# Lightning attention feeding a GELU MLP: second score pair of group 2 four blocks later, loads asked for one pair less far ahead, later visits moved by one to four blocks

## The chip, the cores and the metric

The kernel runs on one core of a Trainium2 chip. The metric is the device time of one execution in microseconds (us). The kernel before has a median of 215.11 us over 6 runs, from 213.0 to 217.37 us.

## The reference

Two stages follow each other. The first is a causal linear attention with decay over 4 batches, 8 heads, 768 positions and 64 features; the second is a two-layer MLP over the 3072 tokens that come out of it:

```python
# attention, per block of positions; Dmask[i, j] = lam^(i-j) where i >= j, else 0
intra    = (q_b @ k_b^T * Dmask) @ v_b
inter    = (q_b * lam^(pos+1)) @ kv_state
out_b    = intra + inter
kv_state = lam^block * kv_state + (k_b * lam^(block-1-pos))^T @ v_b
# MLP: x is the attention output as (3072, 512)
h   = x @ w_in                       # (3072, 2048)
out = gelu_exact(h) @ w_out          # (3072, 512)
```

All inputs and the output are float32. The kernel computes in bf16 with float32 accumulation.

## The kernel before, in words

**Tiling.** The sequence is cut into 6 pieces of 128 positions. A piece of one batch is a chunk (128 positions, all 8 heads), numbered n = piece x 4 + batch, 24 in all. The four chunks of a piece make up group g = 0 to 5, and the MLP works on a whole group (512 tokens) at once.

**The MLP as a list of blocks.** `mlp_blocks(g)` gives the MLP of a group as a list of blocks, each a run of TensorE matmuls. A first-layer block (L263) is 4 matmuls of 128x512 for one of 16 slices of the hidden layer, with a GELU on ScalarE behind it (L265). A second-layer block (L275) is 4 matmuls of a sum of 16; after four blocks ScalarE copies one of the four output tiles (L280) and SyncE stores it (L281). Groups 2 to 4 have 16 + 16 = 32 blocks, group 1 has 33. In groups 2 to 4 the four stores of a group follow blocks 19, 23, 27 and 31; in group 1 they follow blocks 20, 24, 28 and 32.

**Attention as visits.** The attention of group g+1 is done inside the MLP of group g. `visits[(g, i)]` (L432 on) holds what is emitted just ahead of block i. For groups 1 to 4 the line L435 gives four block numbers: at `a0` the scores of the group's first two chunks (`pair_a`, L197), at `a1` those of the other two, at `b` the `quad_b` of all four (inter-chunk part L224, intra-chunk part L230, and a copy into x_t, L236), at `st` the new states (`kv`: matmul L209, then two VectorE operations, L216 and L217). TensorE runs its instructions in the order written, so a visit that isn't ready holds up all blocks behind it.

**What a score needs.** From chunk 8 on, k and q are transposed by DMA. `request(n)` (L366) puts on SyncE's queue a transpose of k (L188) and one of q_hat (L190), and on GpSimd a multiplication q_hat = q * powers of lam (L189). `requests(n)` (L422) does so for chunks n and n+1, then puts on GpSimd their two decayed k (L169, needed only at `st`), and then calls `prefetch`, which issues loads of k, q and v for chunks up to a given number (L66; a cast from float32 to bf16, also issued by GpSimd). So GpSimd's queue is a fixed order of multiplications and load issues, and SyncE's queue a fixed order of transposes and output stores. Both run ahead of TensorE as far as their data and free buffers let them. `requests` is called for chunks 10 and 11 at block 8 of group 1, and after that at blocks `a1 + 1` (for the next group's first pair) and `b + 1` (for its second pair) of groups 1 to 3.

**Buffers.** There are 12 buffers for each of q, k and v; 6 each for q_hat, kT, qT and masked scores; 8 for decayed k; 6 for output tiles. PSUM is split into 4 banks for the MLP ("m") and 4 for attention ("sc"); scores, o_ps and kv_ps take the "sc" banks in turn, each freed by VectorE reading it.

**The start.** Before the MLP of group 0, `keep_warm` (L324) puts matmuls on a constant tile between the first chunks' visits; the last call, L354, emits three of them. The first block of group 0 needs the first slice of w_in, and later ones further slices, which are still being loaded.

Of the kernel before, what the change touches and what calls it, by code (L numbers as in the profile page):

```python
# [15 lines left out]
def kernel(  # L16
# [23 lines left out]
    M = B  # L40
# [23 lines left out]
    def load(n, name):  # L64
        raw[n, name] = qkv_pool.tile([128, H, D], BF16, tag=name, name=f"{name}_t")
        nc.gpsimd.dma_start(raw[n, name], chunk_of(name, n))  # L66
# [89 lines left out]
    def bank(shape, dtype, tag, name):  # L156
        return ps.tile(shape, dtype, tag=tag, name=name, bufs=4)
# [7 lines left out]
    def decay_k(c, eng):  # L165

        if c.so < NB - 1:
            c.k_dec = work_pool.tile([128, H, D], BF16, tag="kd", name="k_dec", bufs=8)
            eng.tensor_mul(c.k_dec, c.k, lam_m[:, :, None].to_broadcast((128, H, D)))  # L169
# [22 lines left out]
    def scores(c):  # L192
        sc_ps = [bank([128, HP, C], F32, "sc", f"sc_ps{hi}") for hi in range(2)]
        for hp in range(HP):
            for hi in range(2):
                p = slice(hi * D, (hi + 1) * D)
                nc.tensor.matmul(sc_ps[hi][:, hp, :], c.kT[p, hp, :], c.qT[p, hp, :], start=True, stop=True)  # L197
        c.sc_m = work_pool.tile([128, HP, 2, C], BF16, tag="sc_m", name="sc_m")
        dmask_r = dmask.rearrange("p (hp hi) i -> p hp hi i", hi=2)
        for hi in range(2):  # L200
            nc.vector.tensor_mul(c.sc_m[:, :, hi, :], sc_ps[hi], dmask_r[:, :, hi, :])  # L201
# [117 lines left out]
    def keep_warm(n, new=True):  # L319

        if new:
            idle_ps[0] = bank([128, 512], F32, "m", "idle_ps")
        for _ in range(n):
            nc.tensor.matmul(idle_ps[0], idle[:, :128], idle, start=True, stop=True)  # L324
# [26 lines left out]
    transposes(live[3])  # L351
    keep_warm(3)
    scores(live[3])
    keep_warm(3)  # L354
    for n in range(M):
        decay_k(live[n], nc.vector)
    make_lam_blk()
# [8 lines left out]
    def request(n):  # L366
        begin(n)
        dma_transposes(live[n])
# [3 lines left out]
    def prefetch(upto):  # L372
        while next_load[0] <= min(upto, NCH - 1):
            for name in "kqv":
                load(next_load[0], name)
            next_load[0] += 1

    def kv(*ns):
        for n in ns:
            next_state(live[n])  # L380
            take_state(live[n])
# [29 lines left out]
    def pair_a(n):  # L411
        for c in (live[n], live[n + 1]):
            scores(c)

    def quad_b(n):
        quad = [live[n + i] for i in range(M)]
        for c in quad:
            inter(c)
        for c in quad:
            intra(c)  # L420

    def requests(n):  # L422
        for m in (n, n + 1):
            request(m)
        for m in (n, n + 1):
            decay_k(live[m], nc.gpsimd)
        prefetch(n + (4 if n == 2 * M + 2 else 5))

    def add(g, i, f):
        visits.setdefault((g, i), []).append(f)  # L430


    for g in range(1, NG - 1):
        n = (g + 1) * M
        a0, a1, b, st = {1: (10, 21, 26, 31), 2: (5, 15, 21, 27)}.get(g, (4, 11, 18, 25))  # L435
        if g == 1:
            add(g, a0 - 2, lambda n=n: requests(n + 2))
        add(g, a0, lambda n=n: pair_a(n))
        add(g, a1, lambda n=n: pair_a(n + 2))
        if g + 2 < NG:  # L440
            add(g, a1 + 1, lambda n=n: requests(n + M))
            add(g, b + 1, lambda n=n: requests(n + M + 2))
        add(g, b, lambda n=n: quad_b(n))
        add(g, st, lambda n=n: kv(n, n + 1, n + 2, n + 3))
# [37 lines left out]
```

## Time and profile before

| | |
|---|---|
| median of 6 runs | 215.11 us (213.0 to 217.37) |
| the profiled execution's own time | 215.03 us |
| its span in the profile | 213.3 us |
| TensorE matmul busy | 203.5 us, 95% of the span |
| GpSimd busy | 102.5 us, all of it before 126.1 us |
| ScalarE, VectorE busy | 87.2 us, 76.1 us |
| granted TensorE clock | full in every slice |

The profile is one execution, 1.7 us shorter than that execution's own time because the span begins with the first instruction and ends with the last. Its page gives busy time by engine, a strip of 40 slices, a chain followed back from the last instruction, and groups of instructions by line. The trace behind it answers for single lines, engines and stretches. Matmuls are pipelined: one of 128x512 shows a duration of 379 ns, but in an unbroken run they follow each other every 0.216 us (16 in 3.45 us on the chain), so a block of four takes 0.86 us. A transpose or a load shows the time of its issue on the queue; the time until its data has landed is told apart.

### The profile page before, as it was taken

The numbers are of one execution on the slowest core, as the hardware profiler recorded it, in microseconds if no ns is written. First come the engines' busy times: TensorE is split into PE (matmuls) and PEld (weight loads), VectorE is DVE, ScalarE is ACT, GpSimd is POOL, SyncE is SP. The second block draws the span as 40 slices with busy tenths as digits, with TensorE's granted clock in tenths as the row PEclk, the third lists the DMA queues.
The fourth block names the chain that finished last, engine by engine and source line by source line (L and its number), as shares of the span: only waits on it lengthen the run. The fifth ranks groups of instructions, "written<-read, shape, count | busy, mean of one in ns | idle before, by whom it ended". The sixth has DMA issues, their size and how long they took to land.

```text
span 213.3 us, 3540 instructions
## 1 busy us (share of the span) xinstructions
PE 203.5 (95%) x1446; PEld 104.7 (49%) x1471; DVE 76.1 (36%) x122; ACT 87.2 (41%) x153; POOL 102.5 (48%) x118
## 2 busy tenths in 40 slices
PE   7888999999999999997999999999999999999994
PEld 2444754556644465443465444645444644444442
DVE  3777130175392334642244544138144120000000
ACT  5663662326657111565102465211456211566121
POOL 7994433892997998999999930000000000000000
PEclk9999999999999999999999999999999999999999
DMA  8999999999999799999999991131200012100112
GB/s 88 137 150 185 207 206 189 154 209 155 177 99 117 87 161 136 185 155 127 187 198 148 213 210 37 24 99 52 98 0 0 3 49 98 49 3 0 49 49 98
DMA packets 100800, 24.48 MB, mean 115 GB/s; under 512 B 92977, under 2 KB 97841, under 8 KB 100785
## 3 DMA queue, kind: packets, MB, share of 16 engines
q0 software_dynamic: 78592, 13.51, 84.8%
q1 hardware_dynamic: 22192, 10.76, 25.0%
q8 instruction: 11, 0.18, 0.4%
q14 instruction: 5, 0.03, 0.1%
HBM read 27.27 MB, written 6.29 MB: 157 GB/s over the span
## 4 chain that ended last, share of the span: by engine, by line
PE 81%; POOL 6%; DMA 6%; DVE 3%; issue 2%; ACT 0%; POOLq 0%
PE o_ps L275 37%; PE h_ps L263 33%; DMA w_in_t<-in_moe_w_in_dram 4%; DMA qT<-q_hat 3%; PE o_ps L230 3%; PE sc_ps L197 2%; PE o_ps L224 2%; PE kv_ps L209 2%; POOL k_t L66 2%; PE o_ps L289 2%; POOL q_t L66 2%; DVE state L217 1%; POOL v_t L66 1%; DVE tmp L216 1%; POOL q_hat L189 1%
## 5 line engine op out<-in xcount | busy, mean ns | idle before, releaser
L263 PE MATMUL h_ps<-x_t,w_in_t 128*128 128x512 bf16 (+2 forms) x422 | 86.0, 355 | 1.0 <-DMA w_in_t<-in_moe_w_in_dram 0.5
L275 PE MATMUL o_ps<-w_out_t,g_t 128*128 128x512 bf16 x355 | 81.0, 379 | 1.3 <-issue 0.9
L265 ACT ACTIVATE g_t<-h_ps 128x512 bf16<-128x512 f32 (+1 forms) x99 | 57.8, 584 | 36.8 <-PE h_ps L263 36.7
L263 PEld LDWEIGHTS <-w_in_t 128*128 128x128 bf16 x432 | 39.2, 98 | 42.2 <-DMA w_in_t<-in_moe_w_in_dram 1.5
L275 PEld LDWEIGHTS <-g_t 128*128 128x128 bf16 x368 | 35.1, 98 | 40.9
L201 DVE TENSOR_TENSOR sc_m<-sc_ps,dmask 128x512 bf16<-128x512 f32 x48 | 30.0, 682 | 37.3 <-PE sc_ps L197 37.3
L280 ACT COPY o_sb<-o_ps 128x512 f32<-128x512 f32 x23 | 13.5, 585 | 72.6 <-PE o_ps L275 69.7
L66 POOL DMA_DIRECT2D k_t<-in_k_dram x24 | 22.1, 921 | 5.9 <-DMA w_in_t<-in_moe_w_in_dram 3.3
L66 POOL DMA_DIRECT2D q_t<-in_q_dram x24 | 21.7, 906 | 3.5 <-DMA w_out_t<-in_moe_w_out_dram 3.4
L66 POOL DMA_DIRECT2D v_t<-in_v_dram x23 | 21.0, 916 | 3.3 <-DMA w_out_t<-in_moe_w_out_dram 1.6
L189 POOL TENSOR_TENSOR q_hat<-q_t,lam_p 128x512 bf16<-128x512 bf16 x16 | 17.3, 1108 | 8.7 <-DMA q_t<-in_q_dram 7.0
L236 DVE CAST x_t<-o_ps 128x512 bf16<-128x512 f32 x16 | 9.9, 683 | 19.1 <-PE o_ps L230 19.1
L169 POOL TENSOR_TENSOR k_dec<-k_t,lam_m 128x512 bf16<-128x512 bf16 x16 | 16.5, 1068 | 0.0
L216 DVE TENSOR_TENSOR tmp<-kv_ps,state 128x512 f32<-128x512 f32 x16 | 10.9, 684 | 14.1 <-PE kv_ps L209 14.1
L217 DVE TENSOR_TENSOR state<-tmp,lam_blk 128x512 bf16<-128x512 f32 x16 | 12.2, 762 | 0.5
L324 PE MATMUL idle_ps<-idle 128*128 128x512 bf16 x29 | 10.6, 476 | 1.2 <-DVE idle L105 1.2
L182 DVE TENSOR_TENSOR qT<-t_ps,lam_q 128x512 bf16<-128x512 bf16 x8 | 5.5, 690 | 14.8 <-PE t_ps L176 14.7
L197 PE MATMUL sc_ps<-qT,kT 64*128 64x128 bf16 x192 | 8.4, 217 | 2.4 <-DMA qT<-q_hat 1.5
L197 PEld LDWEIGHTS <-kT 64*128 64x128 bf16 x192 | 5.7, 94 | 8.1 <-issue 6.0
L230 PE MATMUL o_ps<-sc_m,v_t 128*64 128x128 bf16 x192 | 7.9, 222 | 0.2
L230 PEld LDWEIGHTS <-v_t 128*64 128x64 bf16 x192 | 5.8, 109 | 2.8 <-issue 1.6
L181 ACT COPY kT<-t_ps 128x512 bf16<-128x512 bf16 x8 | 4.7, 586 | 4.6 <-PE t_ps L176 4.6
(41 smaller groups left out, 70.5 us busy)
## 6 DMA issues: line engine op xcount, KB each, us to landing
out_dram<-o_sb SPq DMA_DIRECT2D x23, 256.0 KB, 3.1
k_t<-in_k_dram POOLq DMA_DIRECT2D x24, 128.0 KB, 5.8
q_t<-in_q_dram POOLq DMA_DIRECT2D x24, 128.0 KB, 6.5
v_t<-in_v_dram POOLq DMA_DIRECT2D x23, 128.0 KB, 7.1
w_out_t<-in_moe_w_out_dram POOLq DMA_DIRECT2D x4, 512.0 KB, 16.7
w_in_t<-in_moe_w_in_dram POOLq DMA_DIRECT2D x2, 512.0 KB, 11.6
w_in_t<-in_moe_w_in_dram POOLq DMA_DIRECT2D x2, 384.0 KB, 8.4
v_f<-in_v_dram SPq DMA_DIRECT2D x1, 256.0 KB, 3.5
```

What stands on the lines that cost most here:

```text
L66: nc.gpsimd.dma_start(raw[n, name], chunk_of(name, n))
L169: eng.tensor_mul(c.k_dec, c.k, lam_m[:, :, None].to_broadcast((128, H, D)))
L189: nc.gpsimd.tensor_mul(q_hat, c.q, lam_p[:, :, None].to_broadcast((128, H, D)))
L197: nc.tensor.matmul(sc_ps[hi][:, hp, :], c.kT[p, hp, :], c.qT[p, hp, :], start=True, stop=True)
L201: nc.vector.tensor_mul(c.sc_m[:, :, hi, :], sc_ps[hi], dmask_r[:, :, hi, :])
L216: nc.vector.tensor_add(tmp, kv_ps, states[c.b])
L217: nc.vector.tensor_mul(new, tmp, lam_blk)
L230: nc.tensor.matmul(c.o_ps[hi * D:(hi + 1) * D, hp, :], c.v[:, 2 * hp + hi, :], c.sc_m[:, hp, hi, :], start=(c.so == 0 and hp == 0), stop=T ...
L263: nc.tensor.matmul(h_ps[:, f, :], w, x_t[:, ki, lo:hi], start=(ki == 0 and f == 0), stop=(ki == NK1 - 1), skip_group_check=True)
L265: nc.scalar.activation(g_t[:, kf:kf + n_kf, lo:hi], h_ps, ACT.Gelu)
L275: nc.tensor.matmul(om[io], g_t[:, kf, io * C:(io + 1) * C], w_out_t[:, kf, :], start=(kf == 0), stop=(kf == NK2 - 1))
L280: nc.scalar.copy(o_sb, om[io])
```

## The change

Four things are altered:

- `keep_warm` at L354 emits four matmuls, not three.
- `requests(n)` prefetches up to chunk n+3, that is, only the pair that the next `requests` will ask for. Before, it was n+4 in the first call (n = 10) and n+5 afterwards.
- In group 1, `a1` and `b` are one block later (21 to 22, 26 to 27). In group 2, `a0` is one block later (5 to 6), `a1` four (15 to 19), `b` four (21 to 25), `st` three (27 to 30).
- In groups 3 and 4, `a0` is one block later (4 to 5) and `a1`, `b` and `st` are three later (11, 18, 25 to 14, 21, 28).

`requests` moves with `a1` and `b`. In the order of SyncE's queue, this puts the transposes of chunks 16 and 17 behind the first output store of group 2, those of 18 and 19 behind its second, and those of 22 and 23 behind the first store of group 3; before, each stood one store earlier. On GpSimd, multiplications and bursts of loads change places: each burst of loads issued by `requests` is now the six loads of one pair and stands directly ahead of that pair's two q_hat.

```diff
@@ -351,7 +351,7 @@
     transposes(live[3])
     keep_warm(3)
     scores(live[3])
-    keep_warm(3)
+    keep_warm(4)
     for n in range(M):
         decay_k(live[n], nc.vector)
     make_lam_blk()
@@ -424,7 +424,7 @@
             request(m)
         for m in (n, n + 1):
             decay_k(live[m], nc.gpsimd)
-        prefetch(n + (4 if n == 2 * M + 2 else 5))
+        prefetch(n + 3)
@@ -432,7 +432,7 @@
     for g in range(1, NG - 1):
         n = (g + 1) * M
-        a0, a1, b, st = {1: (10, 21, 26, 31), 2: (5, 15, 21, 27)}.get(g, (4, 11, 18, 25))
+        a0, a1, b, st = {1: (10, 22, 27, 31), 2: (6, 19, 25, 30)}.get(g, (5, 14, 21, 28))
```

## The prediction

> **What bounds the kernel now.** I read the busy row of the page first, then the list of waits, then the stretch of the chain around the one long wait, and then the engines' timelines there.
>
> ```profile
> PE 203.5 (95%) x1446; PEld 104.7 (49%) x1471; DVE 76.1 (36%) x122; ACT 87.2 (41%) x153; POOL 102.5 (48%) x118
> ```
>
> TensorE (PE) is the bound; time can only come from its gaps or from its instructions. The list of waits has these rows for it and for GpSimd (in total, times, longest, in us):
>
> ```profile
> POOL q_hat L189 <- DMA q_t<-in_q_dram: 7.0, 4, 3.3
> ...
> PE sc_ps L197 <- DMA qT<-q_hat: 1.5, 1, 1.5
> ...
> PE h_ps L263 <- DMA w_in_t<-in_moe_w_in_dram: 0.5, 1, 0.5
> ```
>
> After the start, one matmul wait counts: 1.5 us, once, by the scores for a transposed q. The others in TensorE's timeline after it are 0.16 us each. The timeline shows where (start, duration):
>
> ```profile
> 99.62 0.40 PE L197 MATMUL sc_ps<-qT,kT 64*128 64x128 bf16 x8
> 101.55 0.40 PE L197 MATMUL sc_ps<-qT,kT 64*128 64x128 bf16 x8 [1.53 <-DMA qT<-q_hat]
> 101.88 1.04 PE L263 MATMUL h_ps<-x_t,w_in_t 128*128 128x512 bf16 x4
> ```
>
> This is group 2, block 15: chunk 14's scores go at once, chunk 15's wait 1.53 us. The chain leads back through GpSimd:
>
> ```profile
> 90.96 0.95 POOL v_t L66
> 91.91 1.07 POOL q_hat L189
> 92.99 0.92 POOL q_hat L189
> ...
> 95.60 5.81 DMA qT<-q_hat
> 101.41 0.14 issue
> 101.55 0.40 PE sc_ps L197 x8
> ```
>
> GpSimd issued nine loads from 83.96 to 91.8 (for chunks 15, 16 and 17; 14 was long loaded) before it made q_hat of 14 and 15. SyncE then needed three transposes, one after the other:
>
> ```profile
> 93.00 1.19 SPq L190 DMA_TRANSPOSE qT<-q_hat  x1
> 94.28 1.22 SPq L188 DMA_TRANSPOSE kT<-k_t  x1
> 95.60 2.29 SPq L190 DMA_TRANSPOSE qT<-q_hat  x1
> ```
>
> The last landed 5.8 us after its issue, at 101.4. From 101.55 to the end TensorE has no other wait above 0.16 us, so what is saved here should reach the end whole.
>
> **Part by part. 1, the pair four blocks later.** A block takes 4 x 0.216 = 0.86 us, so chunk 15's scores would start without the wait at 101.55 - 1.53 + 4 x 0.86 = 103.5. With qT landing at 101.4 even as it is, the wait is gone with 2.1 us to spare: -1.53 us. No matmul is added; four blocks only change places with 16 score matmuls.
>
> **2, loads one pair less far ahead.** This is the part with a price, as each pair's q_hat now waits for loads issued just ahead of it, and the next burst queues behind that wait. For three bursts of the trace I asked how long a load takes to land (issues at 83-92, 95-101 and 104-111 us):
>
> ```profile
> DMA to landing us min/median/max: 4.9/5.5/6.9
> ...
> DMA to landing us min/median/max: 4.0/7.4/8.1
> ...
> DMA to landing us min/median/max: 6.0/7.4/8.3
> ```
>
> A round on GpSimd is then: six issues (5.3 us; the second chunk's q goes out at +3.5), the landing L, one q_hat (1.04), two decayed k (2.0). Up to 83.96 nothing differs: chunk 13's q_hat waited for its own load before too. Then:
> - Burst for 14, 15 from 83.96: second q at 87.5, L = 5.5 (its own row), q_hat done 94.0. Transpose q of 15 can be issued at 94.1 (before 95.60), landing at 94.1 + 5.8 = 99.9. Needed at 103.5: 3.6 us to spare.
> - Decayed k until 96.0. Burst 16, 17: second q at 99.5, L = 7.4, q_hat done 107.9; its transpose lands about 114. Needed at group 3's block 5: before it was block 4 at 123.02, so 123.02 - 1.53 + 0.86 + 0.28 = 122.6. 8 to spare.
> - Decayed k until 109.9. Burst 18, 19: second q at 113.4, L = 7.4, q_hat done 121.8, issue 121.9, landing 127.7. Needed at block 14: 129.73 - 1.53 + 3 x 0.86 + 0.28 = 131.1. 3.4 to spare, the tightest place.
> - Bursts 20, 21 and 22, 23: q_hat done 135.9 and 147.9, transposes landed 142 and 154, needed at 154.5 and 163.0.
>
> So no new wait: 0. Bounds: three landings in a row (5.5 + 7.4 + 7.4 = 20.3) may sum to 20.3 + 3.4 = 23.7 us before TensorE waits. The largest in the windows, 6.9 + 8.1 + 8.3 = 23.3, just keep inside. Below nothing isn't possible here beyond part 1, since no other wait on q exists.
>
> The Trainium skill ("DMA: Bandwidth & Descriptors", Anatomy of one DMA) prices a load from GpSimd at about 2.0 us plus bytes over 436 GB/s: for 256 KB of float32, 2.6 us. By that rule q_hat would hardly wait, a round would be 5.3 + 2.1 + 2.0 = 9.4 us, and chunk 19's transpose would land 15 us early. By the rows a round takes 12 to 14 us. I take the rows, as these loads lie beside transposes and stores. Both give 0.
>
> **3, SyncE's order.** The transposes of 16, 17 now stand behind group 2's first store (block 19 ends about 104.5, store issued about 105.3), those of 18, 19 behind its second (about 108.7), those of 22, 23 behind group 3's first (about 137). q_hat is later than the store each time except for kT of 16: 0. What queues behind a waiting transpose is stores; the third and fourth of group 2 leave about 123 in place of some time after 116, and six output buffers cover that, as the next tile comes at 137. Stores waited in this way before too: the one row of ScalarE held up by a store (o_sb on "remote", 2.9 us) delayed no matmul. I take 0; were the buffers to run out, a wait of that size is the upper bound, and nothing here can gain.
>
> **4, the other distances.** Moves change the room that VectorE has to free "sc" banks. Group 1, `b` to `st`: 5 to 4 blocks, so the states start at 82.44 in the old times, and the last x_t copy ended at 80.96: hidden, 1.5 us left. Group 2, `b` to `st`, 6 to 5: copies ended 111.06, needed 113.4. Group 2 `st` to group 3 `a0`: 9 to 7 blocks, 6.94 us from first state matmul to first score; VectorE's four additions took 114.27 to 119.48, 5.2 us. Here a rule speaks against the change: "SBUF — State Buffer", Who interferes with whom, says that a VectorE operation with two SBUF inputs (L217 is one) contends with a GpSimd one that reads SBUF, on an exclusive lock. GpSimd now has chunk 18's and 19's q_hat at about 118 and 121, beside the states at 115 to 121. The row of L217 is 691/692/1256 ns (min, median, max): at worst +0.57. By the row two meetings add 1.1 (6.3 < 6.94); by the rule, two full waits of 1.05 add 2.1 (7.3, against 7.2 for the later banks): 0.1 us at most. I take 0. Were the cover gone, each meeting would cost up to 0.57.
>
> **5, one more warm matmul.** +0.216 us at 17 us. TensorE then waits 0.47 us for w_in (it resumes at 19.03), so the wait shrinks to 0.25 and the cost is 0; uncovered it is 0.22.
>
> **Sum.** Span 213.3 - 1.53 = 211.8; the profiled execution 215.03 - 1.53 = 213.5. It lies 0.08 under the median, so I forecast a median of 213.6 us, 0.7% less. About 1% is what a measurement of this kernel can tell from no change.
>
> **Rivals.**
> - Forecast (0.58): 213.6, own range 213.0 to 214.3 (uncovered terms of parts 3 to 5, and the wait's own spread).
> - Larger gain (0.17). Runs spread from 213.0 to 217.37, and a wait on a landing is the kind that varies. If the wait is on average 2.5 us instead of 1.53, the time is 212.6. For it: 213.0 is close to this profile without its wait. Against: the profiled execution is close to the median.
> - No gain (0.16): the wait moves, or something else is late by as much. Chunk 15's landing would have to take 5.5 + 3.6 = 9.1 us, or bank waits of part 4 add up to 1 to 2 us. 215.0, between 214.3 and 216.0. For it: distances got shorter; against: every one of them keeps room in the trace.
> - Slower (0.09): landings slow GpSimd's rounds, and group 3's second pair waits. It decides from a sum of three landings of 23.7 us; the gain is used up at 25.2 (8.4 each), and over 1% is lost from 27.4 (9.1 each). At 9.5 each, the wait is 28.5 - 23.7 = 4.8, the time 215.1 - 1.5 + 4.8 = 218.4. For it: landings grew from 5.5 to 7.4 within the trace, and loads during the weights took up to 16 us. Against: no load from 83 us on needed over 8.3, and bursts are shorter now.
>
> **Range and chances.** The bulk is the forecast and half of each neighbour: 212.2 to 215.9 leaves out the slower case and the ends of two others. Faster by over 1% (under 213.0): the larger gain and a sliver of the forecast, 0.21. Slower by over 1%: 0.09. Within: 0.70.
>
> **What would show it.** Right: no score wait on qT in group 2; q_hat waiting for q_t in every round, with GpSimd's last one ending near 148 rather than 126; TensorE's first second-layer block of group 2 1.5 us plus the moved pair's 0.55 us earlier. Wrong: a wait of L197 at group 3's block 14, a wait of L197 or L209 on VectorE, or a longer gap at 19 us.

## The result and the profile after

The changed kernel has a median of 213.33 us over 17 runs (212.89 to 214.27), the kernel before 214.94 us over 36 runs (213.0 to 218.81). The ratio is 0.9937, with a 95% interval from 0.9918 to 0.9957: 1.6 us or 0.6% less. Here and below the medians are over all runs and the ratios over those in the chip's faster state alone, so a ratio is not exactly the quotient of two medians. The profiled execution took 213.22 us, with a span of 211.5 us (before 215.03 and 213.3). The runs also lie much closer together than before: 1.4 us from first to last in place of 5.8, from half as many runs.

The page's busy row, for the changed kernel:

```profile
PE 203.9 (96%) x1447; PEld 105.4 (50%) x1472; DVE 76.3 (36%) x122; ACT 87.3 (41%) x153; POOL 102.4 (48%) x118
```

The work is the same; the span is shorter. The list of waits now has these rows for the same places (total, times, longest, us):

```profile
POOL q_hat L189 <- issue: 13.8, 7, 3.3
POOL q_hat L189 <- DMA q_t<-in_q_dram: 13.5, 6, 3.8
...
PE h_ps L263 <- DMA w_in_t<-in_moe_w_in_dram: 0.2, 1, 0.2
```

The row of the scores on qT is gone. GpSimd idles 27.3 us ahead of q_hat where it was 8.8 (7.0 and 1.8; for the part called issue the profile names no releaser), and TensorE does not wait for it. TensorE's timeline in group 2, and at group 3's second pair:

```profile
100.31 2.75 PE L275 MATMUL o_ps<-w_out_t,g_t 128*128 128x512 bf16 x12
103.00 0.62 PE L197 MATMUL sc_ps<-qT,kT 64*128 64x128 bf16 x16
...
130.54 0.62 PE L197 MATMUL sc_ps<-qT,kT 64*128 64x128 bf16 x16
```

Both pairs of scores now run as one piece of 16. GpSimd's timeline of the round of chunks 14 and 15 (the second q's load, then the two q_hat):

```profile
88.27 0.92 POOL L66 DMA_DIRECT2D q_t<-in_q_dram  x1
...
90.11 1.04 POOL L189 TENSOR_TENSOR q_hat<-q_t,lam_p 128x512 bf16<-128x512 bf16 x1
94.29 1.04 POOL L189 TENSOR_TENSOR q_hat<-q_t,lam_p 128x512 bf16<-128x512 bf16 x1 [3.15 <-DMA q_t<-in_q_dram]
```

The second q_hat waits 3.15 us for its own load and ends at 95.3, which is later than before (93.9). But the two transposes ahead of its own have left SyncE's queue by then, so its transpose goes out at 95.36 (before 95.60), and it lands 3.4 us faster. SyncE's timeline, and the time from issue to landing of this transpose:

```profile
95.36 1.19 SPq L190 DMA_TRANSPOSE qT<-q_hat  x1
```

```profile
DMA to landing us min/median/max: 2.4/2.4/2.4
```

That is 97.8, 5.5 us ahead of its scores; before it took 5.8 us and landed at 101.4. So the fewer loads did not bring q_hat forward: what came sooner is the landing of its transpose.

### The profile page after: what moved, and what is told of

Same layout as the page of the kernel before. It is cut to its first block, busy times and chain, and to the rows that moved or that the text cites. A ratio compares the mean times of both kernels' runs of the same rounds, so it can differ in the third digit from the quotient of the medians.

```text
span 211.5 us, 3545 instructions
## 1 busy us (share of the span) xinstructions
PE 203.9 (96%) x1447; PEld 105.4 (50%) x1472; DVE 76.3 (36%) x122; ACT 87.3 (41%) x153; POOL 102.4 (48%) x118
## 4 chain that ended last, share of the span: by engine, by line
PE 86%; POOL 5%; DMA 4%; DVE 3%; issue 1%; ACT 0%; POOLq 0%
PE o_ps L275 37%; PE h_ps L263 37%; DMA w_in_t<-in_moe_w_in_dram 4%; PE o_ps L230 3%; PE sc_ps L197 3%; PE o_ps L224 2%; PE kv_ps L209 2%; POOL k_t L66 2%; PE o_ps L289 2%; POOL q_t L66 2%; DVE state L217 1%; DVE tmp L216 1%; PE t_ps L176 1%; POOL v_t L66 1%; POOL w_in_t L90 0%
## 5 line engine op out<-in xcount | busy, mean ns | idle before, releaser
L189 POOL TENSOR_TENSOR q_hat<-q_t,lam_p 128x512 bf16<-128x512 bf16 x16 | 16.8, 1048 | 27.3 <-issue 13.8
L324 PE MATMUL idle_ps<-idle 128*128 128x512 bf16 x30 | 11.1, 482 | 1.2 <-DVE idle L105 1.2
(41 smaller groups left out, 71.5 us busy)
```

The lines of the kernel that those rows point to most:

```text
L189: nc.gpsimd.tensor_mul(q_hat, c.q, lam_p[:, :, None].to_broadcast((128, H, D)))
```

## The experiments

What had to be told apart: which part of the change takes the wait away, whether the other moves bring anything, how much room the new order has, and what made the wait.

**Each part alone.** Ratios are to the kernel before, with 95% intervals; the last column counts runs above 214.3 us. The kernel before ran beside each set of experiments, and the chip was not the same in each: it had a median of 214.96 us (53 of 61 runs above 214.3) beside the four rows from all visits down to group 2's visits alone, and 215.27 us (39 of 43) beside the last three, so a difference of 0.3 us between medians of two sets says nothing.

| kernel | median us (lowest, highest) | ratio | above 214.3 |
|---|---|---|---|
| kernel before, beside the whole change | 214.94 (213.00, 218.81) | 1 | 28 of 36 |
| whole change | 213.33 (212.89, 214.27) | 0.9937 (0.9918 to 0.9957) | 0 of 17 |
| all visits, loads as before | 213.25 (212.75, 214.04) | 0.9904 (0.9865 to 0.9943) | 0 of 8 |
| loads alone | 213.63 (212.91, 216.23) | 0.9949 (0.9926 to 0.9971) | 7 of 22 |
| warm matmul alone | 215.04 (213.85, 218.52) | 1.0005 (0.9981 to 1.0030) | 19 of 22 |
| group 2's visits alone | 213.43 (212.81, 214.80) | 0.9949 (0.9929 to 0.9969) | 4 of 22 |
| group 1's visits alone | 215.20 (213.63, 217.32) | 0.9993 (0.9966 to 1.0019) | 20 of 22 |
| loads and group 1's visits | 213.47 (212.98, 214.23) | 0.9927 (0.9899 to 0.9955) | 0 of 6 |
| group 1's second pair earlier | 214.81 (213.88, 219.42) | 0.9984 (0.9959 to 1.0009) | 17 of 22 |

All visits, without the fewer loads and the warm matmul:

```diff
-        a0, a1, b, st = {1: (10, 21, 26, 31), 2: (5, 15, 21, 27)}.get(g, (4, 11, 18, 25))
+        a0, a1, b, st = {1: (10, 22, 27, 31), 2: (6, 19, 25, 30)}.get(g, (5, 14, 21, 28))
```

> The kernel before with the later visits alone (loads asked for as before, three warm matmuls). Theory A, either part alone is enough: chunk 15's transposed q still lands at about 101.4 us, its scores are due at about 103.4, no wait, ratio 0.993. Theory B, only fewer loads ahead help: the wait stays or moves to another place, ratio 1.000. Theory C, only the later visits help: as A here, ratio 0.993.

The full gain, and a span of 211.5 us as with the whole change. Theory B falls: the visits need no help from the loads.

Loads alone:

```diff
-        prefetch(n + (4 if n == 2 * M + 2 else 5))
+        prefetch(n + 3)
```

> The kernel before with loads asked for one pair less far ahead, visits unchanged. Theory A: as in the changed kernel, GpSimd finishes chunk 15's q_hat at about 95.3 and its transpose, with fewer loads in the queues, lands at about 97.8 to 100, due at 99.9: no wait or 0.1 us, ratio 0.993. Theory C, only the later visits help: the wait of 1.5 us stays in group 2, or group 3's second pair (due at 128.3) waits, ratio 1.000 or more. Theory B: 0.993.

The gain is there, so theory C falls as well. Group 2's scores at the old block 15 no longer wait. But the profiled execution of this kernel, 214.88 us long, had a wait in a place where the profile of the kernel before shows none (TensorE's timeline):

```profile
72.35 0.40 PE L197 MATMUL sc_ps<-qT,kT 64*128 64x128 bf16 x8
73.87 0.40 PE L197 MATMUL sc_ps<-qT,kT 64*128 64x128 bf16 x8 [1.12 <-DMA qT<-q_hat]
...
101.18 0.62 PE L197 MATMUL sc_ps<-qT,kT 64*128 64x128 bf16 x16
```

This is group 1's second pair (chunks 10 and 11). GpSimd's and SyncE's work up to there is the same in both kernels: the transpose of chunk 11's q was issued at 70.25 and took 3.5 us to land here, against 69.14 and 2.4 us in the profile of before, where it landed at 71.5 for scores due at 72.4. So that place had less than 1 us of room, and an execution can use it up. Here it was used up further ahead: GpSimd's first load after its four decayed k went out at 59.16, against 58.06 before, and TensorE had already waited 0.46 us for one of these decayed k at 56.8, a third place where the kernel can wait. Why GpSimd was behind in this execution stays open. That these waits came first is not what saved group 2: its transposed q landed at 98.0 (issued at 94.29, 3.7 us), and without them its scores would have needed it at 99.9.

The warm matmul alone:

```diff
-    keep_warm(3)
+    keep_warm(4)
     for n in range(M):
```

> The kernel before with a fourth warm matmul alone. Hidden by the wait for w_in at 19 us: ratio 1.000, and that wait falls from 0.47 to about 0.25 us. If it is not hidden: +0.22 us, ratio 1.001. If it is part of the gain: 0.997 or less.

No effect that can be measured. Its profiled execution had no wait for w_in at all at 19 us, while that of the whole change had 0.24 where 0.25 was expected: the wait itself varies from one execution to the next (up to 0.8 us in the profile of another experiment). This profile, with the old visits and loads, also has a wait of 1.09 us at group 1's second pair, and none in group 2 (TensorE's timeline):

```profile
71.99 0.40 PE L197 MATMUL sc_ps<-qT,kT 64*128 64x128 bf16 x8
73.48 0.40 PE L197 MATMUL sc_ps<-qT,kT 64*128 64x128 bf16 x8 [1.09 <-DMA qT<-q_hat]
...
100.80 0.62 PE L197 MATMUL sc_ps<-qT,kT 64*128 64x128 bf16 x16
```

In it chunk 15's transpose went out at 95.36 and landed 5.5 us later, at 100.9, for scores that came at 101.1. Without the delay in group 1 they would have come at 99.9 and waited.

Group 2's visits alone:

```diff
-        a0, a1, b, st = {1: (10, 21, 26, 31), 2: (5, 15, 21, 27)}.get(g, (4, 11, 18, 25))
+        a0, a1, b, st = {1: (10, 21, 26, 31), 2: (6, 19, 25, 30)}.get(g, (4, 11, 18, 25))
```

> The kernel before with group 2's four visit numbers alone moved as in the change. Theory A: the whole gain is this one wait, so ratio 0.993 as with all visits moved. Rival: the shifts in groups 1, 3 and 4 bring part of it, then 0.995 to 0.998 here.

0.9949 is between the two expectations, and its interval holds the first and a part of the second. Most of the gain or all of it comes from group 2's visits; 4 of 22 runs above 214.3 where the whole change has none fit a place left in group 1, but don't show it.

**Two places, one delay.** The next three kernels were made to see how the two places go together. Group 1's visits alone:

```diff
-        a0, a1, b, st = {1: (10, 21, 26, 31), 2: (5, 15, 21, 27)}.get(g, (4, 11, 18, 25))
+        a0, a1, b, st = {1: (10, 22, 27, 31), 2: (5, 15, 21, 27)}.get(g, (4, 11, 18, 25))
```

> The kernel before with group 1's visits alone one block later (22 and 27). Two profiles of other kernels with the old visits show a wait of 1.1 us at group 1's second pair in place of the one in group 2. Theory D, the two places share one delay (a wait at the first makes the second later by as much, so the larger counts): group 2's wait of 1.5 us stays or comes back, ratio 1.000. Theory E, they add up over the executions: ratio 0.997 here.

No gain. The interval doesn't exclude theory E's 0.997, but the profile shows the wait back in group 2, after a small one left in group 1 (TensorE's timeline):

```profile
74.28 0.40 PE L197 MATMUL sc_ps<-qT,kT 64*128 64x128 bf16 x8 [0.20 <-DMA qT<-q_hat]
...
102.76 0.40 PE L197 MATMUL sc_ps<-qT,kT 64*128 64x128 bf16 x8 [1.63 <-DMA qT<-q_hat]
```

GpSimd was late in this execution too (that first load at 59.63). One block is 0.86 us, so a wait of about 1.1 us shrinks to about 0.2: the later visit makes the wait in group 1 small, it does not rule it out.

Fewer loads and group 1's visits together (both diffs above):

> The kernel before with loads asked for one pair less far ahead and group 1's visits one block later. Theory D: the loads remove group 2's wait and the later visit group 1's, so the time is the changed kernel's (213.3 us, ratio 0.993), with few executions above 214.3, where the loads alone had 7 of 22. If group 1's place is not the cause of that spread: 213.6 us and as wide as with the loads alone.

213.47 us, none of 6 runs above 214.3. That fits theory D, but it is weak: the medians (213.63 us with the loads alone) don't differ beyond what two sets can, and at a rate of 7 in 22 six runs without a high one would still come up about one time in ten. What speaks for group 1's place more strongly is that the whole change and the visits alone, which have the later visit too, have no high run in 25, and the kernel with six multiplications below, which has it as well, two in 17, against 11 in 44 for the loads alone and group 2's visits alone.

Group 1's second pair two blocks earlier, requests in place:

```diff
-        add(g, a1, lambda n=n: pair_a(n + 2))
+        add(g, a1 - (2 if g == 1 else 0), lambda n=n: pair_a(n + 2))
```

> The kernel before with group 1's second pair of scores two blocks earlier, everything else in place (its requests too). The scores of chunk 11 are then due at 70.6 us, its transposed q lands between 71.5 and 73.8: a wait of 0.9 to 3.1 us there. Theory D, the larger of two waits counts: group 2's wait falls by as much, time 215 us up to a wait of 1.6, at most 216.5; ratio 1.000 to 1.007. Theory E, waits add: 0.9 to 3.1 us more than before, 215.9 to 218.1 us.

The visit is 1.7 us earlier and waits, and the kernel is no slower. TensorE's timeline:

```profile
71.49 0.40 PE L197 MATMUL sc_ps<-qT,kT 64*128 64x128 bf16 x8 [0.90 <-DMA qT<-q_hat]
...
100.53 0.62 PE L197 MATMUL sc_ps<-qT,kT 64*128 64x128 bf16 x16
```

The interval ends at 1.0009, below all that theory E allows (1.004 at least). This profile does not show why the second wait is missing: GpSimd was some 1.7 us ahead in this execution (its second q_hat of the pair ended at 92.2, not 93.9), and chunk 15's transposed q landed at 99.1, in time even for scores without the delay. The times of 22 runs say that the waits do not add up, and the profile of the warm matmul alone shows how: there the delay in group 1 is what covers group 2's landing.

**What makes the wait.** In `requests(12)`, two more chunks are loaded ahead:

```diff
-        prefetch(n + (4 if n == 2 * M + 2 else 5))
+        prefetch(n + {2 * M + 2: 4, 3 * M: 7}.get(n, 5))
```

> The kernel before with loads asked for two more chunks further ahead at one place: fifteen loads in place of nine stand ahead of the q_hat of chunks 14 and 15, none in the next round. Theory A, loads ahead of q_hat in GpSimd's queue make the wait: six issues of 0.87 us more, so the wait of 1.5 us grows to between 3.3 and 6.7 us (depending on how long the transpose takes to land), 216.5 to 220 us. Rival, the landing of the transposes among busy queues makes it: 1.5 us or less, 215 us or less.

220.0 us, and all four runs between 218.9 and 221.4. TensorE's timeline in group 2:

```profile
104.42 0.61 PE L197 MATMUL sc_ps<-qT,kT 64*128 64x128 bf16 x8 [4.69 <-DMA qT<-q_hat]
105.39 0.61 PE L197 MATMUL sc_ps<-qT,kT 64*128 64x128 bf16 x8 [0.35 <-DMA qT<-q_hat]
```

Six more issues on GpSimd put the two q_hat 5.6 us later (97.47, before 91.84) and brought 5.0 us of wait in place of 1.5. So loads that stand ahead of q_hat in GpSimd's queue make a wait, and the rival, by which busy queues alone make it, falls. That does not make the landing unimportant: with fewer loads the second q_hat was no earlier (95.3 in the changed kernel, 94.3 with the loads alone, 93.9 before), and what took the wait away is a transpose that left SyncE's queue somewhat sooner and landed in 2.4 or 3.7 us. The 1.5 us are the two together, nine issues and a landing of 5.8 us. The time grew by more than the wait did, which the last section takes up.

**How much room the new order has.** Six or twelve multiplications, their results unused, ahead of the loads of chunks 18 and 19 in the changed kernel (line added inside `requests`; twelve in the second kernel):

```diff
+        if n == 4 * M:
+            for _ in range(6):
+                late = work_pool.tile([128, H, D], BF16, tag="late", name="late", bufs=2)
+                nc.gpsimd.tensor_mul(late, live[n].k, lam_m[:, :, None].to_broadcast((128, H, D)))
         prefetch(n + 3)
```

> The changed kernel with six further multiplications of 1.05 us (6.3 us, their results unused) on GpSimd just ahead of the loads of chunks 18 and 19. Theory A, room as the trace of the changed kernel gives it (transposed q of chunk 19 lands at 124.6, its scores are due at 130.8, 6.2 us of room): no wait or 0.1 us, time as the changed kernel. Rival, room as the prediction worked it out (3.4 us): a wait of 2.9 us at group 3's second pair, about 216.2 us.

> The changed kernel with twelve such multiplications (12.6 us) at the same place. Theory A: 12.6 - 6.2 = 6.4 us of wait at group 3's second pair if the loads take as long to land as in the changed kernel (219.7 us), about 3.4 us (216.7 us) if they land as fast as those of chunks 20 and 21 (4.8 us). Rival, room of 3.4 us: 9.2 us, 222.5 us. If GpSimd's order does not set TensorE's waits at all: 213.3 us.

With six: 213.19 us over 17 runs (212.77 to 215.02, two of them above 214.3), no wait. GpSimd's second q_hat of this pair then started at 123.97 and not 121.15, only 2.8 us later for some 6 us of added work: the later loads landed sooner (5.8 us at most, not 9.2), and took up the rest. So the missing wait does not decide between the two expectations, as 2.8 us is less than 3.4; but the transposed q landed at 127.4 for scores due at 131.5, with 4.1 us still to spare. With twelve: 218.09 us over 12 runs (215.32 to 219.56), so the cover is gone. The profiled execution, one of the shorter ones with 216.50 us, shows where (TensorE's timeline):

```profile
132.36 0.40 PE L197 MATMUL sc_ps<-qT,kT 64*128 64x128 bf16 x8
134.02 0.40 PE L197 MATMUL sc_ps<-qT,kT 64*128 64x128 bf16 x8 [1.26 <-DMA qT<-q_hat]
```

This execution had two smaller waits in group 1 as well (0.34 us for a transposed q and 0.6 us for a decayed k), which made these scores later and their wait smaller. Against the changed kernel, chunk 19's transpose went out 9.25 us later (131.47), its scores were due 1.8 us later, and 1.3 us of wait is left: a room of some 6.1 us, as theory A had it from the trace. The median, 4.8 us above the changed kernel's, is not a wait alone. The four runs whose mean granted clock was 0.999 or 1.0 took 215.32 to 216.50 us, 2.0 to 3.2 us more; the other eight, with a clock of 0.984 to 0.992, 217.19 to 219.56 us. So GpSimd's order does set TensorE's waits here, once q is some 6 us later; the last section comes back to the clock.

## Why the prediction was right, and where it was off

The forecast was 213.6 us or 0.7% less, the measured median is 213.33 us, 0.6% less. The main term was right; the reading that it was the only wait was not, and one landing was sized too long.

- **Part 1, the pair four blocks later** held. The profile gave -1.53 us; the span fell by 1.8 and the median by 1.6. The idle figure understates the wait a little, because it is counted from the modelled end of the last matmul (99.62 + 0.40). Eight score matmuls of an unbroken 16 take 0.28 us, so the next would have begun at 99.90, and 101.55 - 99.90 is 1.65.
- **"After the start, one matmul wait counts"** was the step that was wrong. It was true of the one execution that the profile shows, and not of the kernel. Group 1's second pair is as near the edge: two profiles with the old visits there wait 1.1 us at it. Moving group 1's `a1` by one block was costed only by its bank distances, but it takes most of this second wait away. That the sum came out was luck in this respect: the two waits share one delay and don't add, which the prediction did not know.
- **Part 2, loads less far ahead** was priced at 0, and that holds; but it also removes group 2's wait alone, and the prediction took that gain for part 1 only. Its working already had chunk 15's transpose landing at 99.9 instead of 101.4, for scores due at 100.0 in the old place. It landed at 97.8. The mis-sized term is the transpose's landing: 5.8 us was carried over from a moment with loads in flight, and it was 2.4 us in the new order, for chunks 15 and 19 alike. For the same reason the tightest place, group 3's second pair, had 6.2 us of room where 3.4 was worked out (landing 124.6, due 130.8), and the two kernels with added multiplications bear it out: 4.1 us left after a delay of 2.8, and some 6.1 in the one that waited.
- **The landing of loads** came out right in sum, not one by one: 6.0 us for chunk 15's q, 4.3 for chunk 17's, 9.2 for chunk 19's (predicted 5.5, 7.4, 7.4). The last is above every landing that the prediction had found from 83 us on (8.3), but the three add to 19.5 us, under its 20.3 and well under its bound of 23.7. The slower rival had the right mechanism: the twelve multiplications are that rival made by hand. That both cost 4.8 us is chance, as the rival's figure is wait alone and the measured one is wait and lost clock.
- **Parts 3 and 4**: nothing. No wait of L209 on VectorE and none of ScalarE on a store delayed TensorE. Beside GpSimd's q_hat, one of the four state operations of group 2 took 0.94 us in place of 0.69. With the visits alone, where GpSimd multiplies and issues without a pause there, the four took 1.28, 1.05, 1.17 and 0.82 us, more than the two meetings of 0.57 that were allowed for, and the scores behind them had no wait either.
- **Part 5**, the warm matmul, cost nothing, alone and in the profile.
- **The larger gain** as a rival had the right reason (a wait on a landing varies), and the runs of before are indeed wide; but their median sat at the profile's value (214.94 and 215.03).
- Of what was to be seen in the profile, q_hat's wait in every round was too much: the first q_hat of chunks 14 and of 16 started without one, as their loads had landed by the end of the burst. GpSimd's last q_hat ended at 144.5, not 148. Group 2's first second-layer block came 2.4 us earlier (100.31, before 102.75), where 2.1 was named.

## What to carry to other kernels

A queue that issues loads and also makes operands has an order, and each load put ahead of an operand delays it by its issue time, here 0.87 us, and a transpose issued among loads in flight landed up to 3.4 us later than one issued after them; loads further ahead are no gain where the next pair's own are in time. One profile shows one execution: a place that meets its operand with less than a microsecond to spare waits in other executions, so look for the small margins beside the waits. Two waits for one late queue don't add up, since the first makes the second's consumer later; removing only one of them can bring nothing (group 1's here) or nearly everything (group 2's).

## What was not expected of the hardware

A long wait costs more than itself. In the kernel with fifteen loads ahead of q_hat, the granted TensorE clock fell during the wait of 4.69 us. The stretches, in one answer each row of which gives PE, PEld, DVE, ACT and POOL busy time, then granted clock, DMA share and GB/s:

```profile
95.00:99.70 4.70, 4.70 (x22) 1.94 (x20) 0.00 (x0) 3.18 (x6) 4.70 (x6) 1.00 3.07 150
99.70:104.42 4.72, 0.04 (x1) 0.03 (x1) 0.00 (x0) 0.60 (x1) 4.72 (x5) 0.93 2.47 135
104.42:106.00 1.58, 1.22 (x17) 0.79 (x18) 0.96 (x2) 0.00 (x0) 1.58 (x3) 0.50 1.09 374
106.00:108.00 2.00, 2.00 (x6) 0.67 (x6) 1.52 (x3) 0.14 (x1) 2.00 (x3) 0.50 0.94 146
108.00:110.00 2.00, 2.00 (x6) 0.76 (x5) 0.00 (x0) 0.46 (x1) 2.00 (x4) 0.50 2.01 165
110.00:112.00 2.00, 2.00 (x9) 0.84 (x8) 0.00 (x0) 0.00 (x0) 2.00 (x3) 0.85 1.90 141
```

At half clock from 104.42 to 110.00 and 0.85 until 112.00, some 0.5 x 5.58 + 0.15 x 2.0 = 3.1 us of work are lost (an estimate from these rows). The span grew by 6.3 us (213.3 to 219.6): 3.5 us more of waits (5.04 - 1.53) and about 2.8 that the clock explains. Waits of 0.9 to 1.6 us, as in the kernels above, left the clock at 1.00 around them (in group 1's visits alone, 99 to 110 us with its wait of 1.63). The Trainium skill ("TensorE: Matmul & The Clock Gate", The HAM clock gate) puts the idle time after which the clock halves at about 3.4 us, with a return after as long a busy stretch. The fall fits it, about 4 us after the last matmul (the clock was still 1.00 at 103.7 and 0.50 from 104.0); the return took some 6 us here, with a gap of 0.35 us inside. It bears on the slower rival, whose price of 4.8 us of waiting should have had such a term added.

The kernel before may pay this price at times. Of its 132 runs beside the experiments, 28 have a mean granted clock of 0.992 or less, and they took 216.6 to 219.3 us. The kernels in which group 2's wait is gone (the changed one, the one with six multiplications, all visits, group 2's visits, loads alone, loads and group 1's visits) have one such run in 92, and the kernel with fifteen loads ahead has four in four. A wait at group 2 that is now and then long enough to bring the clock down would look like this; no trace of such a run was kept, so it is not shown.

The second thing is how much a transpose's landing goes with what else is in the DMA queues: 2.4 us when issued after a burst of loads had landed, 5.8 us when issued with loads in flight. A load issued right behind it goes with a longer landing too: chunk 11's q took 3.4 to 3.6 us in the four profiles in which GpSimd's next load was issued 0.2 us after its transpose, and 2.4 us in the eight in which that load came 1.0 us or more after it. No experiment varied this alone, so that the loads cause it is argued, not shown.
